# Float64 weights converted by a scaled read, a shift and an addition, and the second layer's slot stage issued straight behind the experts

## The chip, the cores and the metric

One core of a Trainium2 chip runs the whole program in one launch. The metric is device time in microseconds. The kernel before took 983.55 us as the median of 3 runs (982.73 to 985.5).

## The reference, cut to what matters

Three layers follow one another. The attention (8 batches, 8 heads, 576 tokens, 64 per head) gives x, 4608 x 512. A soft mixture of 8 experts mixes the tokens into 32 slots, runs each expert on its 4 slots, and mixes the slots back. A last layer squares its hidden values:

```
logits = x @ phi                                  # 4608 x 32
slot_input = softmax(logits, over tokens).T @ x   # 32 x 512
slot_out[e] = relu(slot_input[e] @ w1[e]) @ w2[e] # 8 experts, 512 x 1024 and 1024 x 512
y = softmax(logits, over slots) @ slot_out        # 4608 x 512
h = y @ w_in                                      # w_in 512 x 2048, float64
out = (s * relu(h)**2 + b) @ w_out                # w_out 2048 x 512, float64
```

`w_in` and `w_out` arrive in float64, so the kernel reads them as pairs of 32-bit words and makes float32 of them itself.

## The kernel before, in words

The attention runs from an order written out by hand: each step has a time `tau` in a table (`SLOT`), `at` collects the steps, and `run` issues them in the order of their times. Engines take what is issued to them in that order.

The last layer is not computed as `(c @ slot_out) @ w_in`. The kernel first forms M = slot_out @ w_in, 32 x 2048, and later h = c @ M, with c the 4608 x 32 softmax. M is called `mf` in float32, and `mst` as high and low float16 parts, with a power of two as scale. This is **M's stage** (from line 885): `slot_rows` brings the experts' sum `so` to the other axis (`sos`, `sop`, `soT`); `slots(i)` makes 256 columns of M at a time (matmul `m`, copy `part`, matmul `n` that adds four parts, copy into `mf`); then come a scale for M (`msum`), the split into `mst` (`parts`), a bound on the outputs by 16 transposes of `mf` and a maximum (`mm`, `mu`), and the scales `sk` and `bk`.

The **main loop** (from line 980) goes over 12 groups of 384 tokens and 16 slices f of 128 hidden columns: `stage_h` (matmul h, relu on ScalarE), `stage_g` (square and scale on VectorE), `stage_r` (high and low parts, ScalarE and VectorE), and `stage_o` (9 float16 matmuls of 512 columns), issued `LAG` = 4 steps behind `stage_h`. `stage_e` writes 384 rows out.

The **weights** come in 1 MB pieces, called keys: 8 of `wi` (w_in), 8 of `wo` (w_out), 16 of `w1` and 16 of `w2`. `load_w` issues a `w1` or `w2` key as two transfers of 512 KB on SyncE's queue; a load waits there until the place it goes to is free. Places: 3 (`wpost`) in the room that the attention leaves, 1 (`wright`) in the room that the routing leaves, the place of every expert key that has been used (`used`), and the places of the odd `wi` and `wo` keys once they have been converted (`split`; these loads show as `w2h`). `advance` issues a load for each place as it is named.

The **conversion** of a key is a generator: `from_f64` has three pieces, then the pieces of its `finish` list follow (one for `wi`; value, power, power2, high, low for `wo`). One call of `convert(most)` issues one piece of each conversion in flight and takes up a new one if fewer than `most` are in flight. Seven calls stand in the end of the attention's order, one behind each of the 32 expert keys, and the rest follow the experts in a loop, ahead of M's stage. The 16 keys' conversions, in order: wi0 to wi7, wo0 to wo7. The pieces are numbered below as wi2:3 for the third piece of wi2.

Of the kernel before, what the change touches and what calls it, by code (L numbers as in the profile page):

```python
# [13 lines left out]
U32 = mybir.dt.uint32  # L14
AF = mybir.ActivationFunctionType
# [25 lines left out]
def fused_kernel(  # L41
# [569 lines left out]
    def from_f64(w, pool, finish):  # L611
# [12 lines left out]
        yield  # L624
        DVE.scalar_tensor_tensor(out=f, in0=m, scalar=2.0 ** -20, in1=f, op0=ALU.mult, op1=ALU.add)
        yield
        DVE.scalar_tensor_tensor(out=e, in0=h32, scalar=-0x80000000, in1=e, op0=ALU.bitwise_and, op1=ALU.bitwise_or)
        yield
        for fn in finish:
            fn(f, e.bitcast(F32))  # L630
            yield
# [30 lines left out]
    P["cv"] = later(ph2, "cv", 2)  # L662
    wpost = places(ph2, "wpost", NPOST, reuse_waits="tile")
    ready, todo, active = set(), [], []
# [36 lines left out]
    def split_wo(i):  # L701
# [3 lines left out]
        def value(u, s):  # L705
            DVE.tensor_tensor(out=u, in0=u, in1=s, op=ALU.mult)

        def power(u, s):
            for h in range(2):
                ACT.activation(out=s[:, 512 * h:512 * h + 512], in_=u[:, 512 * h:512 * h + 512], func=AF.Abs, bias=eps,  # L710
                               accum_out=wsum[:, 2 * i + h:2 * i + h + 1])

        def power2(u, s):

            DVE.tensor_scalar(out=wpow[:, 2 * i:2 * i + 2].bitcast(I32), in0=wsum[:, 2 * i:2 * i + 2].bitcast(I32),
                              scalar1=0x7F800000, scalar2=0x7F800000, op0=ALU.bitwise_and, op1=ALU.bitwise_xor)
            ACT.mul(wpow[:, 2 * i:2 * i + 2], wpow[:, 2 * i:2 * i + 2], 2.0 ** 13)

# [9 lines left out]
        def low(u, s):  # L728
# [5 lines left out]
            if i % 2:  # L734
                empty.append(split(home["wo", i], i))
                advance()

        return from_f64(wt["wo", i], P["cv"], [value, power, power2, high, low])

    def conv_in(i):  # L740
# [3 lines left out]
        def finish(u, s):  # L744
            DVE.tensor_tensor(out=to, in0=u, in1=s, op=ALU.mult)
            have.add(i)
            if i % 2:
                empty.append(split(home["wi", i], i))
                advance()

        return from_f64(wt["wi", i], P["cv"], [finish])
# [30 lines left out]
    CMOST = 2  # L782
# [4 lines left out]
    for t in (O["rp"] - 0.01, O["rp"] - 0.005, O["tl"] + 0.1, O["re"] + 0.3, O["re"] + 0.35, O["rx"] + 0.2, O["rx"] + 0.3):  # L787
        at(z + t, 7, convert, 1)
# [12 lines left out]
    with tc.manual_schedule():  # L801
# [63 lines left out]
        while todo or active:  # L865
            convert(CMOST)
# [18 lines left out]
    with tc.manual_schedule():  # L885

        pm = ph3.enter_context(tc.tile_pool(name="pm", bufs=3, space=PSUM, reuse_waits="tile"))
        mdone = set()
        soT = e1.tile([128, 4, 32], F32, name="soT")

        def slot_rows():
# [6 lines left out]
            DVE.tensor_copy(soT, sop[:, 0:128].rearrange("p (c n) -> p c n", c=4))  # L898

        def slots(i):  # L900
# [8 lines left out]
            (DVE.tensor_copy if i % 2 else ACT.copy)(part, ps)  # L909
# [8 lines left out]
        msum = e1.tile([128, 12], F32, name="msum")  # L918
        sb_abs = e1.tile([128, 2], F32, name="sb_abs")
        ACT.activation(out=sb_abs[:, 0:1], in_=s_sb, func=AF.Abs)  # L920
        ACT.activation(out=sb_abs[:, 1:2], in_=b_sb, func=AF.Abs)
        slot_rows()
        ctrans(0, pm, "n")
        gens = [slots(i) for i in range(8)]
        for i in range(10):
            if i < 8:
                next(gens[i])
            if i >= 2:
                next(gens[i - 2], None)

        DVE.tensor_reduce(out=msum[:, 8:9], in_=msum[:, 0:8], axis=AX, op=ALU.add)
        gp = pm.tile([128, 512], F32, tag="n", name="n")
        PE.matmul(gp[:, 0:128], msum[:, 8:9].to_broadcast([128, 128]), idF, start=True, stop=True)
        DVE.tensor_reduce(out=msum[:, 9:10], in_=gp[:, 0:128], axis=AX, op=ALU.max)
        for n, x in ((10, 0x7F800000), (11, 0)):
            DVE.tensor_scalar(out=msum[:, n:n + 1].bitcast(I32), in0=msum[:, 9:10].bitcast(I32), scalar1=0x7F800000, scalar2=x,
                              op0=ALU.bitwise_and, op1=ALU.bitwise_xor)
        ACT.mul(msum[:, 10:11], msum[:, 10:11], 2.0 ** 13)
        ACT.mul(msum[:, 11:12], msum[:, 11:12], 2.0 ** -28)

        def parts(x0, x1):
            ACT.activation(out=mst[:, x0:x1], in_=mf[:, x0:x1], func=AF.Copy, scale=msum[:, 10:11])
            DVE.scalar_tensor_tensor(out=mst[64:128, x0:x1], in0=mf[64:128, x0:x1], scalar=msum[64:128, 10:11],
                                     in1=mst[64:128, x0:x1], op0=ALU.mult, op1=ALU.subtract)
            mdone.update(range(x0 // 256, x1 // 256))

        parts(0, 512)


        mt = pm.tile([128, 512], F32, tag="m", name="m")  # L950
        for f in range(16):
            PE.transpose(mt[:, 32 * f:32 * f + 32], mf[0:32, 128 * f:128 * f + 128], idF[0:32, 0:32])
# [128 lines left out]
```

## Time and profile before

| | |
|---|---|
| time, median of 3 | 983.55 us |
| profiled execution | 982.77 us |
| its span | 981.1 us, mean granted TensorE clock 0.973 |
| PE busy | 879.0 us (90%) |
| DVE busy | 703.6 us (72%) |
| ACT busy | 604.1 us (62%) |
| POOL busy | 286.5 us (29%) |

PE is TensorE's matmul, DVE VectorE, ACT ScalarE, POOL GpSimd, SP SyncE. All times count from the start of the span. A timeline row gives start, duration, engine, line, operation, output and inputs, shapes and count; in brackets, the idle time of the engine before it and what ended that. A windows row gives a stretch and its length, then each engine's busy time with its count of instructions, the granted PE clock (1.00 is full), the DMA engines' busy share, and GB/s. A groups row gives line, engine, operation, names, shapes and count, then busy time, the mean ns of one, and the idle time before them. Durations of neighbours overlap a little: two 1024-column VectorE instructions of 1.22 us start 1.14 us apart.

### The profile page before, as it was taken

To read this page: it belongs to the slowest core of one execution; us is meant where nothing else is said; L and a number is where in the kernel's file an instruction comes from. 1 tells how busy PE (TensorE), PEld (TensorE's weight loads), DVE (VectorE), ACT (ScalarE), POOL (GpSimd) and SP (SyncE) were. 2 spreads that over 40 slices of the span, in tenths; PEclk is the share of its full clock that TensorE was granted. 3 is DMA by queue.
4 is the path that set the end of the run, shared out by engine and by line. 5 is a ranking of instruction groups with operands and counts; after the bars stand their busy time and mean duration, and the time that the engine had idled before them with its cause. 6 is when DMAs were issued, how large, how long until landed. Compare 5 with 4: busy or idle time off the path is not lost.

```text
span 981.1 us, 20487 instructions
## 1 busy us (share of the span) xinstructions
PE 879.0 (90%) x8052; PEld 515.1 (53%) x8052; DVE 703.6 (72%) x1269; ACT 604.1 (62%) x1040; POOL 286.5 (29%) x224
## 2 busy tenths in 40 slices
PE   3899989988999988876785699999999999999998
PEld 2677767767777767761110334444444444444443
DVE  5798979888899879848889566565555565565553
ACT  2677767777677767753377655555555555565553
POOL 6576756665566646652000000000000000000000
PEclk9999999999999999987999789999999999999999
DMA  4544544444434434075995000001000100010001
GB/s 113 130 91 118 129 109 101 102 120 115 110 81 123 123 106 112 15 302 217 410 400 214 1 1 33 11 23 33 33 1 32 33 32 2 33 33 1 33 33 32
DMA packets 150927, 91.73 MB, mean 94 GB/s; under 512 B 127472, under 2 KB 127792, under 8 KB 150832
## 3 DMA queue, kind: packets, MB, share of 16 engines
q1 hardware_dynamic: 150832, 90.44, 30.7%
q8 instruction: 63, 1.03, 0.4%
q14 instruction: 32, 0.26, 0.1%
HBM read 80.81 MB, written 9.44 MB: 92 GB/s over the span
## 4 chain that ended last, share of the span: by engine, by line
PE 58%; DVE 21%; ACT 11%; DMA 4%; issue 3%; POOL 3%; SPq 0%; DVEq 0%; POOLq 0%; ACTq 0%
PE o L1015 13%; PE o L1014 13%; PE o L1016 13%; DVE vl L356 5%; PE s L378 4%; DVE mm L292 4%; ACT pc L383 4%; PE h L986 3%; ACT ph L255 3%; PE tp L268 2%; DMA w<-in_moe_w_dram 2%; PE s L303 2%; DVE me L292 2%; PE pv L416 1%; DVE kql L262 1%
## 5 line engine op out<-in xcount | busy, mean ns | idle before, releaser
L262 POOL TENSOR_TENSOR pl<-pc,ph 128x896 f16<-128x896 f32 (+1 forms) x128 | 232.4, 1817 | 150.0 <-ACT ph L255 82.6
L994 DVE SCALAR_TENSOR_TENSOR g<-r,sk 128x384 f32<-128x384 f32 x192 | 119.4, 622 | 128.2 <-ACT r L988 126.7
L988 ACT ACTIVATE r<-h,msum 128x384 f32<-128x384 f32 x192 | 111.4, 581 | 156.4 <-PE h L986 155.3
L383 ACT ACTIVATE pc<-s 128x896 f32<-128x896 f32 (+1 forms) x128 | 110.6, 864 | 75.1 <-PE s L378 48.0
L1002 DVE SCALAR_TENSOR_TENSOR rl<-g,bk,rh 128x384 f16<-128x384 f32 x192 | 117.9, 614 | 8.0 <-ACT rh L1000 6.7
L1000 ACT ACTIVATE rh<-g,bk 128x384 f16<-128x384 f32 x192 | 116.5, 607 | 2.2 <-DVE g L994 2.2
L255 ACT CAST ph<-pc 128x896 f16<-128x896 f32 (+1 forms) x128 | 113.4, 886 | 4.1
L292 DVE TENSOR_REDUCE mm<-s 128x2 f32<-128x1024 f32 (+3 forms) x128 | 101.8, 817 | 7.3 <-PE s L303 7.1
L766 POOL TENSOR_TENSOR c<-lgs,mc 128x192 f32<-128x192 f32 x6 | 3.0, 508 | 345.6 <-DVE mc L764 345.6
L416 PE MATMUL pv<-vh,ph 128*128 128x65 f16 x960 | 102.5, 196 | 1.2 <-DVE xt L432 1.0
L418 PE MATMUL pv<-vh,pl 128*128 128x65 f16 x960 | 101.0, 194 | 1.3 <-POOL pl L262 1.3
L417 PE MATMUL pv<-vl,ph 128*128 128x64 f16 x960 | 101.4, 193 | 0.0
L416 PEld LDWEIGHTS <-ph 128*128 128x128 f16 x960 | 86.6, 98 | 23.0 <-issue 6.3
L1016 PEld LDWEIGHTS <-rl 128*128 128x128 f16 x576 | 56.4, 98 | 68.7 <-DVE rl L1002 0.7
L1014 PEld LDWEIGHTS <-rh 128*128 128x128 f16 x576 | 56.5, 98 | 66.6 <-issue 0.3
L418 PEld LDWEIGHTS <-pl 128*128 128x128 f16 x960 | 88.7, 98 | 1.6 <-POOL pl L262 1.5
L417 PEld LDWEIGHTS <-ph 128*128 128x128 f16 x960 | 88.6, 99 | 0.0
L1015 PEld LDWEIGHTS <-rh 128*128 128x128 f16 x576 | 56.5, 98 | 58.3 <-issue 0.6
L262 DVE TENSOR_TENSOR kql<-tp,kq 128x512 fp32r<-128x512 f32 (+1 forms) x96 | 57.5, 599 | 29.2 <-ACT kq L284 28.2
L268 PE MATMUL tp<-idF,rqk 128*128 128x128 f32 x320 | 57.9, 298 | 22.0 <-DVE kql L262 9.6
L303 PE MATMUL s<-kq 64*128 64x64 f32 (+4 forms) x384 | 55.3, 336 | 20.6 <-DVE me L292 14.6
L378 PE MATMUL s<-kq 64*128 64x128 f32 (+3 forms) x384 | 70.4, 363 | 0.8
(236 smaller groups left out, 1967.7 us busy)
## 6 DMA issues: line engine op xcount, KB each, us to landing
w<-in_moe_w_dram SPq DMA_DIRECT2D x44, 512.0 KB
w2h<-in_moe_w_dram SPq DMA_DIRECT2D x20, 512.0 KB
rqk<-in_k_dram SPq DMA_DIRECT2D x64, 128.0 KB
rqk<-in_q_dram SPq DMA_DIRECT2D x64, 128.0 KB
rv<-in_v_dram SPq DMA_DIRECT2D x64, 128.0 KB
wi<-in_moe_w_in_dram SPq DMA_DIRECT2D x8, 1024.0 KB
wo<-in_moe_w_out_dram SPq DMA_DIRECT2D x8, 1024.0 KB
out_dram<-ob SPq DMA_DIRECT2D x32, 256.0 KB
```

The source lines that it names most:

```text
L255: ACT.copy(o, i)
L262: eng.tensor_tensor(out=o, in0=i, in1=h, op=ALU.subtract)
L292: DVE.tensor_reduce(out=o, in_=i, axis=AX, op=ALU.max)
L383: ACT.activation(out=pc[:, :, 0:w], in_=st.pop(("ps", p, c))[:, :, 0:w], func=AF.Exp, scale=scale)
L416: PE.matmul(o, a, vh[:, 2 * sl + h, 0:65], start=(c == 0 and n == 0), stop=False)
L417: PE.matmul(o[:, 0:64], a, vl[:, 2 * sl + h, :], start=False, stop=False)
L418: PE.matmul(o, l, vh[:, 2 * sl + h, 0:65], start=False, stop=(c == 3 and n == len(UNIT[c]) - 1))
L994: DVE.scalar_tensor_tensor(out=g0, in0=r, scalar=sk[:, f:f + 1], in1=r, op0=ALU.mult, op1=ALU.mult)
L1002: DVE.scalar_tensor_tensor(out=rl, in0=g0, scalar=bk[:, f:f + 1], in1=rh, op0=ALU.add, op1=ALU.subtract)
L1014: PE.matmul(o, rh[:, 128 * i:128 * i + 128], hl[f][0], start=(f == 0), stop=False)
L1015: PE.matmul(o, rh[:, 128 * i:128 * i + 128], hl[f][1], start=False, stop=False)
L1016: PE.matmul(o, rl[:, 128 * i:128 * i + 128], hl[f][0], start=False, stop=(f == 15))
```

## The change

`from_f64` reads the upper word as a float32 and multiplies it by 2^-112 on ScalarE, shifts the bits left by 3 and puts the sign back (VectorE); the lower word, scaled by 2^-52 in bfloat16 (ScalarE), is multiplied by the power of two of the value, taken from the upper 16 bits (VectorE); `value` or `finish` then adds the two. Up to three conversions are in flight instead of two, and two instead of one ahead of the experts, where six calls stand instead of seven. The place of an odd key is named free behind the second piece instead of the last. The loop that issued the rest of the conversions is gone: M's stage is issued behind the last expert key with `convert` between its pieces and behind it. In M's stage the 16 transposes stand behind each piece of `mf`; M's scale comes from the same maximum and minimum as the bound, by one pair of matmuls, and the sums of absolute values `msum` are gone; all `part` copies are ScalarE's; `mst` is split in pieces, most of them between the first steps of the main loop, whose first `stage_o` stand 2 to 4 steps behind `stage_h`.

```diff
-        m = pool.tile([128, n], I32, tag="cvm", name="cvm", bufs=1)
-        e = pool.tile([128, n], I32, tag="cve", name="cve")
-        f = pool.tile([128, n], F32, tag="cvf", name="cvf")
-        DVE.tensor_scalar(out=e, in0=h32, scalar1=1, scalar2=21, op0=ALU.logical_shift_left, op1=ALU.logical_shift_right)
-        DVE.tensor_scalar(out=m, in0=h32, scalar1=0xFFFFF, scalar2=None, op0=ALU.bitwise_and)
-
-        ACT.activation(out=f, in_=l32, func=AF.Copy, scale=2.0 ** -52, bias=1.0)
-        ACT.activation(out=e, in_=e, func=AF.Relu, bias=m896, scale=2.0 ** 23)
+        g = P["cv"].tile([128, n], I32, tag="cvg", name="cvg")
+        l = P["cv"].tile([128, n], BF16, tag="cvl", name="cvl")
+        e = P["cv"].tile([128, n], BF16, tag="cve", name="cve", bufs=1)
+        gf = g.bitcast(F32)
+        ACT.activation(out=gf, in_=h32.bitcast(F32), func=AF.Copy, scale=2.0 ** -112)
+        ACT.activation(out=l, in_=l32, func=AF.Copy, scale=2.0 ** -52)
         yield
-        DVE.scalar_tensor_tensor(out=f, in0=m, scalar=2.0 ** -20, in1=f, op0=ALU.mult, op1=ALU.add)
+        DVE.tensor_scalar(out=g, in0=g, scalar1=3, scalar2=None, op0=ALU.logical_shift_left)
+        DVE.scalar_tensor_tensor(out=g, in0=h32, scalar=-0x80000000, in1=g, op0=ALU.bitwise_and, op1=ALU.bitwise_or)
+        if key[1] % 2:
+            empty.append(split(home[key], key[1]))
+            advance()
         yield
-        DVE.scalar_tensor_tensor(out=e, in0=h32, scalar=-0x80000000, in1=e, op0=ALU.bitwise_and, op1=ALU.bitwise_or)
+
+        up = g.bitcast(I16).rearrange("p (n t) -> p n t", t=2)[:, :, 1]
+        DVE.tensor_scalar(out=e.bitcast(I16), in0=up, scalar1=-128, scalar2=None, op0=ALU.bitwise_and)
+        DVE.tensor_tensor(out=l, in0=l, in1=e, op=ALU.mult)
         yield
...
-            DVE.tensor_tensor(out=u, in0=u, in1=s, op=ALU.mult)
+            DVE.tensor_tensor(out=u, in0=u, in1=s, op=ALU.add)
...
-    CMOST = 2
+    CMOST = 3
...
-    for t in (O["rp"] - 0.01, O["rp"] - 0.005, O["tl"] + 0.1, O["re"] + 0.3, O["re"] + 0.35, O["rx"] + 0.2, O["rx"] + 0.3):
-        at(z + t, 7, convert, 1)
+    for t in (O["rp"] - 0.01, O["rp"] - 0.005, O["tl"] + 0.1, O["re"] + 0.3, O["rx"] + 0.2, O["rx"] + 0.3):
+        at(z + t, 7, convert, 2)
...
-        while todo or active:
-            convert(CMOST)
...
-            (DVE.tensor_copy if i % 2 else ACT.copy)(part, ps)
+            ACT.copy(part, ps)
...
-            ACT.activation(out=part, in_=ps, func=AF.Abs, bias=eps, accum_out=msum[:, i:i + 1])
-            (ACT.copy if i % 2 else DVE.tensor_copy)(mf[:, 256 * i:256 * (i + 1)], ps)
+            (DVE.tensor_copy if i < 7 else ACT.copy)(mf[:, 256 * i:256 * (i + 1)], ps)
+            yield
+            for f in (2 * i, 2 * i + 1):
+                PE.transpose(mt[:, 32 * f:32 * f + 32], mf[0:32, 128 * f:128 * f + 128], idF[0:32, 0:32])
...
+        for i in range(11):
+            for j in (i, i - 2, i - 3):
+                if 0 <= j < 8:
+                    next(gens[j], None)
+            if i < 10:
+                convert(CMOST)
+        while len(summed) < 8:
+            convert(CMOST)
...
+        extremes(0, 16)
...
+        for n in range(2):
+            PE.matmul(gp[:, 128 * n:128 * n + 128], top[:, n:n + 1].to_broadcast([128, 128]), idF, start=True, stop=True)
+        DVE.tensor_reduce(out=top, in_=gp[:, 0:256].rearrange("p (a n) -> p a n", a=2), axis=AX, op=ALU.max)
...
-        parts(512, 2048)
...
+        part_hi(0, 256)
...
+        part_lo(0, 256)
...
+        part_hi(256, 512)
...
+        at(0.9, part_lo, 256, 512)
+        for x in range(512, 2048, 512):
+            at(x / 128 - 2.6, part_hi, x, x + 512)
+            at(x / 128 - 1.8, part_lo, x, x + 256)
+            at(x / 128 - 0.8, part_lo, x + 256, x + 512)
+
+        for n in range(8):
+            at(n + 1.3, convert, CMOST)
...
-            at(n + LAG + .05, stage_o, g, f)
+            lag = min(LAG, 2 + n / 4) + .05
+            at(n + lag, stage_o, g, f)
```

## Rows read from the trace of the kernel before

**Rows 1.** Windows, by stage: first experts, second experts, conversions, M's stage, main loop.

```profile
454.30:488.50 34.20, 27.32 (x116) 4.19 (x108) 31.58 (x38) 12.54 (x11) 0.00 (x0) 0.96 1.00 397
492.00:531.40 39.40, 32.33 (x128) 4.60 (x128) 34.78 (x43) 29.04 (x51) 0.00 (x0) 1.00 0.96 368
531.40:543.20 11.80, 0.00 (x0) 0.00 (x0) 10.54 (x15) 9.05 (x17) 0.00 (x0) 0.68 0.00 0
543.20:567.30 24.10, 17.09 (x116) 8.92 (x117) 14.30 (x38) 15.07 (x42) 0.00 (x0) 0.71 0.00 1
567.30:980.00 412.70, 409.03 (x1949) 188.66 (x1947) 237.41 (x426) 228.03 (x425) 8.79 (x15) 1.00 0.07 24
```

**Rows 2.** Timeline of PE, last expert key to the first `stage_o`.

```profile
530.30 1.05 PE L853 MATMUL so<-w,hTz 128*32 128x512 f32 x4 [0.25 <-DMA w<-in_moe_w_dram]
...
543.80 1.92 PE L897 MATMUL m<-I,sos 128*128 128x32 f32 x8 [12.46 <-ACT sos L894]
...
549.64 0.64 PE L905 MATMUL m<-wi,soT 128*32 128x256 f32 x8
...
550.84 0.64 PE L905 MATMUL m<-wi,soT 128*32 128x256 f32 x8
...
558.16 1.18 PE L952 MATMUL m<-idF,mf 32*128 32x32 f32 x16
...
562.33 0.80 PE L965 MATMUL n<-idF,mu 128*128 128x128 f32 x2 [2.99 <-DVE mu L963]
...
567.33 0.63 PE L1014 MATMUL o<-wo_0s,rh 128*128 128x512 f16 x1
```

**Rows 3.** Groups of DVE by shape, 430:567 us; L994 from 600:970.

```profile
L706 DVE TENSOR_TENSOR cvf<-cvf,cve 128x1024 f32<-128x1024 f32 x8 | 9.8, 1225 | 0.3
...
L627 DVE SCALAR_TENSOR_TENSOR cve<-wo,cve 128x1024 int32<-128x1024 int32 x8 | 9.7, 1218 | 0.0
...
L619 DVE TENSOR_SCALAR cve<-wo 128x1024 int32<-128x1024 int32 x8 | 5.5, 686 | 0.0
...
L730 DVE SCALAR_TENSOR_TENSOR wo_4s<-cvf,wpow,wo_4s 128x512 f16<-128x512 f32 x4 | 2.8, 743 | 0.0
...
L994 DVE SCALAR_TENSOR_TENSOR g<-r,sk 128x384 f32<-128x384 f32 x173 | 107.5, 621 | 118.2 <-ACT r L988 116.9
```

**Rows 4.** Groups of ACT by shape, 488:560 us; L988 from 600:970.

```profile
L622 ACT ACTIVATE cvf<-wo 128x1024 f32<-128x1024 uint32 x8 | 9.2, 1152 | 0.0
...
L710 ACT ACTIVATE cve<-cvf,eps 128x512 f32<-128x512 f32 x16 | 11.3, 710 | 2.8 <-DVE cvf L706 2.8
...
L725 ACT ACTIVATE wo_4s<-cvf,wpow 128x512 f16<-128x512 f32 x4 | 2.7, 714 | 0.1
...
L988 ACT ACTIVATE r<-h,msum 128x384 f32<-128x384 f32 x173 | 100.5, 581 | 142.0 <-PE h L986 140.8
```

**Rows 5.** Timeline of DVE ahead of the experts.

```profile
442.08 0.32 DVE L509 COPY d<-s 128x160 f32<-128x160 f32 x1
...
445.19 0.75 DVE L520 SCALAR_TENSOR_TENSOR acc<-acc,f,s 128x512 f32<-128x512 f32 x1 [0.41 <-PE s L518]
...
450.82 0.35 DVE L771 TENSOR_REDUCE sc<-c 128x6 f32<-128x192 f32 x1 [2.59 <-ACT c L768]
...
451.72 0.28 DVE L808 COPY slotT<-stp 128x128 f32<-128x128 f32 x1
```

**Rows 6.** Timeline of ACT in the same stretch.

```profile
441.50 0.23 ACT L542 ACTIVATE W<-W 128x32 f32<-128x32 f32 x1 [0.58 <-DVE W L541]
```

**Rows 7.** Timeline of POOL in the same stretch.

```profile
446.90 3.02 POOL L795 MEMSET hTz<- 128x2304 f32 x1 [15.27 <-DVE ssum L527]
```

**Rows 8.** Windows of the core, the 4 us after slotT.

```profile
452.00:456.00 4.00, 3.95 (x20) 0.99 (x24) 4.00 (x5) 0.89 (x2) 1.28 (x2) 0.50 0.23 84
```

**Rows 9.** Timeline of DVE in M's stage, two reductions.

```profile
560.55 0.69 DVE L958 TENSOR_REDUCE mmax<-m 128x16 f32<-128x512 f32 x1
...
563.16 0.29 DVE L966 TENSOR_REDUCE mu<-n 128x1 f32<-128x128 f32 x1 [0.89 <-PE n L965]
```

More of the change, by code (lines that the diff above doesn't have):

```diff
@@ L661, in fused_kernel @@
     e2 = later(ctx, "e2", 2)
-    P["cv"] = later(ph2, "cv", 2)
+    P["cv"] = later(ctx, "cv", 3)
     wpost = places(ph2, "wpost", NPOST, reuse_waits="tile")
-    ready, todo, active = set(), [], []
+    ready, summed, todo, active = set(), set(), [], []
     toload = list(wseq[NPRE:])
@@ L733, in low @@
             ready.update((2 * i, 2 * i + 1))
[L734 to L738, printed above, removed]
+        return from_f64(("wo", i), [value, power, power2, high, low])
     def conv_in(i):
@@ L744, in finish @@
         def finish(u, s):
-            DVE.tensor_tensor(out=to, in0=u, in1=s, op=ALU.mult)
+            DVE.tensor_tensor(out=to, in0=u, in1=s, op=ALU.add)
             have.add(i)
[L747 to L751, printed above, removed]
+        return from_f64(("wi", i), [finish])
     def convert(most):
@@ L897, in slot_rows @@
                 PE.matmul(sop[:, 32 * c:32 * c + 32], sos[:, 128 * c:128 * c + 128], I4, start=True, stop=True)
-            DVE.tensor_copy(soT, sop[:, 0:128].rearrange("p (c n) -> p c n", c=4))
+            ACT.copy(soT, sop[:, 0:128].rearrange("p (c n) -> p c n", c=4))
         def slots(i):
@@ L917, in fused_kernel, with small @@
         mf = mstp.tile([128, 2048], F32, name="mf")
-        msum = e1.tile([128, 12], F32, name="msum")
         sb_abs = e1.tile([128, 2], F32, name="sb_abs")
-        ACT.activation(out=sb_abs[:, 0:1], in_=s_sb, func=AF.Abs)
-        ACT.activation(out=sb_abs[:, 1:2], in_=b_sb, func=AF.Abs)
+        def small(name, n=16):
+            return e1.tile([128, n], F32, name=name)
+        mm, mn, bound, gpow, sk, bk, rs_ = (small(n) for n in ("mmax", "mmin", "bound", "gpow", "sk", "bk", "rscale"))
@@ L922, in fused_kernel @@
+        top, power, inv, fm, fo = (small(n, 2) for n in ("top", "power", "inv", "fm", "fo"))
         slot_rows()
         ctrans(0, pm, "n")
-        gens = [slots(i) for i in range(8)]
[L925 to L952, printed above, removed]
-        def small(name, n=16):
-            return e1.tile([128, n], F32, name=name)
-        mm, bound, gpow, sk, bk, rs_, mu = (small(n) for n in ("mmax", "bound", "gpow", "sk", "bk", "rscale", "mu"))
-        DVE.tensor_reduce(out=mm, in_=mt.rearrange("p (f n) -> p f n", n=32), axis=AX, op=ALU.max)
+        mt = pmt.tile([128, 512], F32, name="mt")
@@ new lines, in extremes @@
+        def extremes(f0, f1):
+            x = mt[:, 32 * f0:32 * f1].rearrange("p (f n) -> p f n", n=32)
+            DVE.tensor_reduce(out=mm[:, f0:f1], in_=x, axis=AX, op=ALU.max)
+            DVE.tensor_reduce(out=mn[:, f0:f1], in_=x, axis=AX, op=ALU.min)
+        gens = [slots(i) for i in range(8)]
+        for i in range(11):
[4 more added lines that the diff above has]
+                convert(CMOST)
@@ new lines, in fused_kernel @@
+        while len(summed) < 8:
+            convert(CMOST)
+        for n, c in enumerate((s_sb, b_sb)):
+            DVE.tensor_scalar(out=sb_abs[:, n:n + 1].bitcast(I32), in0=c.bitcast(I32), scalar1=0x7FFFFFFF, scalar2=None,
+                              op0=ALU.bitwise_and)
+        DVE.tensor_scalar(out=gpow.bitcast(I32), in0=wsum.bitcast(I32), scalar1=0x7F800000, scalar2=None, op0=ALU.bitwise_and)
+        extremes(0, 16)
+        DVE.scalar_tensor_tensor(out=mn, in0=mn, scalar=-1.0, in1=mm, op0=ALU.mult, op1=ALU.max)
@@ new lines, in fused_kernel, with part_hi, part_lo @@
+        DVE.tensor_scalar(out=fm, in0=inv, scalar1=2.0 ** 13, scalar2=None, op0=ALU.mult)
+        def part_hi(x0, x1):
+            ACT.activation(out=mst[:, x0:x1], in_=mf[:, x0:x1], func=AF.Copy, scale=fm[:, 0:1])
+        def part_lo(x0, x1):
+            DVE.scalar_tensor_tensor(out=mst[64:128, x0:x1], in0=mf[64:128, x0:x1], scalar=fm[64:128, 0:1],
+                                     in1=mst[64:128, x0:x1], op0=ALU.mult, op1=ALU.subtract)
+            mdone.update(range(x0 // 128, x1 // 128))
@@ L975, in fused_kernel @@
-        DVE.tensor_scalar(out=mu[:, 3:4], in0=mu[:, 3:4], scalar1=2.0 ** -28, scalar2=None, op0=ALU.mult)
-        parts(512, 2048)
+        part_hi(256, 512)
     ph3.close()
@@ L987, in stage_h @@
             r = e3.tile([128, 384], F32, tag="r", name="r")
-            ACT.activation(out=r, in_=hps, func=AF.Relu, scale=msum[:, 11:12])
+            ACT.activation(out=r, in_=hps, func=AF.Relu, scale=fo[:, 0:1])
             rr_[g, f] = r
```

34 lines of the change are left out of this document (18 added, 16 removed).

## The prediction, made before the changed kernel ran

> **What bounds the kernel now.** I read the windows by stage first. In the main loop PE is busy 409.03 of 412.70 us at clock 1.00 while DVE and ACT have over 170 us each to spare [rows 1]; its length is fixed by its matmuls, and the change leaves those as they are. So what counts is when its first `stage_o` starts: 567.33 [rows 2]. Ahead of it lie two stretches in which PE is not the limit. Both expert halves run with the DMA engines at 0.96 to 1.00 of their time and 368 to 397 GB/s: the 32 MB of expert weights set the pace. Then PE stands still for the whole of 531.4 to 543.2, DVE busy 10.54 of 11.80, with no transfer at all; then M's stage, 24.1 us with PE busy 17.09 at a mean clock of 0.71 [rows 1]. The PE timeline says what it waited for: the last expert key ends at 531.35, and the next matmul comes at 543.80, after 12.46 us of waiting for ACT's `sos` [rows 2]. `sos` needs only `so`, which is complete at 531.35; it stands in ACT's queue behind the rest of the conversions. That wait is what the change is aimed at.
>
> **The conversions.** Per `wi` key VectorE has two one-source instructions and three two-source ones. A two-source pass over 1024 columns is 1.22 us (L706, L627), a one-source pass 0.69 (L619) [rows 3]; less the 0.08 by which neighbours overlap, 1.14 and 0.60, so 3 x 1.14 + 2 x 0.60 = 4.62 us. After: the shift 0.60, the sign 1.14, the mask on 16-bit words, the product in bfloat16, the sum 1.14. Neither the mask nor the product has a row. I bound the mask by 0.3 (half of L619, were half the bytes half the time) and 1.14, and the product by 0.66 (L730, a two-source pass over half the columns [rows 3]) and 1.14. I take 0.60 and 1.14, the rows with the same count of columns and of sources. The pair is then 1.74 (0.96 to 2.28) and the key 4.62 again: by these rows the new arithmetic saves VectorE nothing. ACT has two passes per key as before, 1.15 each [rows 4]; I take 0 for the bfloat16 output, between 0.4 gained (L710, half the columns) and nothing.
>
> No row here has both inputs in 16 bits. The Trainium skill (VectorE: DVE Perf Modes, "The perf-mode tier table") puts `tensor_tensor` on bfloat16 in SBUF at twice the float32 rate; by that the product would be 0.60 by estimate, and the time below would be 1.1 us less. The same page ("What auto-detection actually checks") gives the 16-bit packing only to steps of 1, so the mask, which reads every other word, gains nothing by its width.
>
> **What is in flight when the experts end.** Counting the calls of `convert`: before, the call behind the 32nd key issues wo2:7 and wo3:4, and wo4 to wo7 follow the experts. After, with three in flight, it issues wo6:4 and wo7:3. What is left for M's stage is wo6's and wo7's power, power2, high and low and wo7's value; all eight later calls in the loop issue nothing. Whether the engines keep up: VectorE work from the start of the experts to those pieces is six `wi` keys (27.7), six `wo` keys at 4.62 + 1.41 for low (L730 twice, overlapped) + 0.17 for power2 (37.2), wo6 4.62, wo7 3.48, some 1.0 of small things, together 74.0. One thing gets later: `hs`, between the two halves, stands in ACT's queue behind abs of wo1, which needs 27.7 + 2 x 4.62 + 1.74 of that VectorE work, so it comes at about 497, where the first half's keys are in by 458.5 + 11 x 2.64 = 487.6 (next part); before, the second half had begun by 492.0 [rows 1]. This delays PE by 5 to 7 us, not the transfers, which have free places past that point. PE's four matmuls on 512 KB take 1.05 [rows 2] against 1.32 of transfer at 397 GB/s, so over the 32 halves left it can make up 8.6. I cost it at nothing; if the places ran out, it would be up to 7.
>
> **The start of the experts.** Two conversions ahead of the experts cost something. wi1's two ACT passes (2.1) now stand between the routing's ACT work and the exponential W. ACT was idle 0.58 before W at 441.50 [rows 6], so it was free at 440.92; W starts 440.92 + 2.1 = 443.0, 1.5 late, and d, behind W on VectorE, too. d ends at 443.9 instead of 442.4 [rows 5]. Then VectorE does wi0:3 and wi1:2, 1.74 + 1.74, until 447.4, and acc comes there: 2.2 later than 445.19. POOL's clearing of hTz, which waits for the sums behind acc and lasts 3.02 [rows 7], ends at 452.1. VectorE meanwhile has wi0:4, wi1:3 and wi1:4 (4.0) from 449.0 to 453.0; then come the maximum, POOL's subtraction and ACT's exponential (1.2 in sum), so sc starts at 454.2 instead of 450.82. slotT ends 1.18 after sc's start in both: 455.4 instead of 452.0. **3.4 us late.**
>
> Against that, wi1's place is named free two pieces earlier, ahead of `wright`, and its load of one key needs only wi1:2, done at 447.4. So five keys instead of four can land before the experts start (two at 1.05 MB / 397 GB/s = 2.64 us each, 447.4 to 452.7). The load stream can only go on once the first key is used. Before, 84 GB/s in 452 to 456 [rows 8] is 0.34 MB, 0.85 us at full rate, so it resumed at 455.15, 3.1 behind slotT. After it resumes 3.4 later with 2.64 less to load. **The last expert key ends at 531.35 + 3.4 - 2.64 = 532.1.** VectorE, started at 455.4, has its 74.0 done at 529.4: hidden with 2.7 to spare. If it waits on ACT 0.7 per `wo` key, it is 3 late; wo6's abs on ACT, behind the first `part`, is needed only then, so nothing is lost.
>
> **M's stage.** `sos` 0.7 (as L710), `sop` 1.92 at half clock and so about 0.96 at full (PE comes straight from the experts at 1.00 [rows 1]), soT 0.4: first `m` at E + 2.05, with E = 532.1. `m` to `m` with an `n` between is 1.20 (549.64 to 550.84), 16 transposes 1.18 [rows 2]. PE alone would end at E + 2.05 + 9.6 + 1.2 = E + 12.8. But ACT has all the `part` copies (0.37 each), with four abs (0.71) and four high (0.71 [rows 4]) between the first four of them, some reads of sums too: part 4 comes at E + 10.2. Behind it are four `n`, one `m` and the transposes; the two pairs of low on VectorE (1.41 each) stand ahead of the copies that transposes wait for, another 0.8. I get the last transpose at **E + 15.2 = 547.3**.
>
> From there: two reductions of 0.69 instead of one, then small instructions of 0.2. Before, 560.55 to 562.33 (one reduction, five small), 0.83 to 563.16, and on [rows 9, 2]. After: 1.4 + 6 x 0.2 = 2.6 to the matmuls, 0.9, a reduction of twice the columns 0.4, three small ones 0.6, `part_hi` 0.45, `part_lo` 0.48 (a quarter of a 1024-column pass and its fixed part), h 0.5, r 0.58 and g 0.62 [rows 4, 3], and 1.2 of the second r, a `part_hi` and rh on ACT: 8.4. First `stage_o` at **555.7**, 11.6 earlier. Two h (0.17 each) then follow inside the loop that stood ahead of it before: 11.3. Later pieces of `mst` are 3 us of VectorE and 2 us of ACT over 14 steps, with over 0.9 us of slack per step [rows 1]: nothing.
>
> The sum is 982.77 - 11.3 = **971.5** on the profiled execution's time, 0.8 below the median of the runs shown; a measurement here tells about 0.3% (3 us) from no change.
>
> **Rivals.** *Conversions reach into M's stage* (0.17): with the mask and product at 1.14 each, slotT is 1.1 later and VectorE 14 x 0.54 = 7.6 more, so with the 2.7 spare gone and 3 of waits about 8 late at E; abs on ACT then holds part 1 some 5 us. 971.5 + 1.1 + 5 = 977.6. For it: VectorE was 88 to 92% busy in the experts already [rows 1]. Against: both prices at their upper ends.
>
> *The experts start no later* (0.13): if ACT's passes or VectorE's pieces find gaps I have not seen, and the key gained counts in full, 971.5 - 3.4 = 968.1; a cheaper mask and product go the same way (1.8). For it: VectorE idles 2.59 ahead of sc [rows 5]. Against: engines keep their order.
>
> *M's stage isn't freed* (0.05): VectorE's 78 us in all plus 5.6 of waits end at 540.5, and if M's pieces only come then, M without conversions takes 13.0, the rest 8.4: 561.9, so 977.4.
>
> *Slower* (0.03): VectorE's new pair at 3.3 us. It works 14 keys on it ahead of the experts' end, 22 us more, so `m`'s second piece waits till 555, and o starts at about 576: 992. It decides from about 2.7 us for the pair, above the bound of 2.28.
>
> **Chances.** The forecast with 968.5 to 974.5 has 0.60, and 0.02 is left for within 0.3%. The range 966 to 978 takes in the first three rivals. Faster 0.95, same 0.02, slower 0.03.
>
> **What would show it.** PE's wait for `sos` gone: matmul L897's successor within 2 us of the last expert key, at a clock of 1.00. slotT at 455, the last key at 532, the last transpose 15 us behind it, first `stage_o` at 556; the loop's length as before. The mask at 0.69 and the product at 1.22 or 0.69. Wrong would be: idle PE behind the experts, a product over 1.3, or a stall in the loop's first steps.

## The result and the profile after

The changed kernel takes **974.59 us** (median of 4 runs, 973.07 to 975.57) against 984.52 for the kernel before on the same chip, a ratio of 0.9899 (0.988 to 0.9917): faster by 9.9 us. The forecast was 971.5, 966 to 978. The profiled execution is the longest of the four, 975.57, where that of the kernel before was the shortest of its own; its span is 973.9 against 981.1: 7.2 less.

Busy times and the granted clock, from the page of the kernel after:

```profile
span 973.9 us, 20478 instructions
PE 874.5 (90%) x8052; PEld 515.9 (53%) x8052; DVE 700.2 (72%) x1275; ACT 599.0 (62%) x1025; POOL 285.3 (29%) x224
PEclk9799999999999999996979899999999999999999
```

No engine has noticeably less to do (PE 4.5 us less, DVE 3.4, ACT 5.1). What changed is how the work stands. The PE timeline of the kernel after, from the last expert key to the main loop (rows as in [rows 2]):

```profile
532.20 1.05 PE L859 MATMUL so<-w2h,hTz 128*32 128x512 f32 x4 [0.22 <-DMA w2h<-in_moe_w_dram]
533.94 1.08 PE L902 MATMUL m<-I,sos 128*128 128x32 f32 x8 [0.69 <-ACT sos L899]
...
541.70 0.70 PE L917 MATMUL n<-part,J 128*128 128x256 f32 x2 [0.84 <-ACT part L914]
...
549.47 0.31 PE L921 MATMUL mt<-idF,mf 32*128 32x32 f32 x2 [0.23 <-ACT mf L918]
551.57 1.62 PE L966 MATMUL n<-idF,top 128*128 128x128 f32 x4 [1.80 <-DVE top L959]
555.38 0.82 PE L999 MATMUL h<-ct,mst 128*128 128x384 f16 x2 [2.19 <-DVE mst L978]
...
558.14 0.63 PE L1027 MATMUL o<-wo_0s,rh 128*128 128x512 f16 x1
```

The 12.46 us of idle PE behind the last key [rows 2] are 0.69 now. From the last key's end (533.25) to the end of the last transpose (549.78) it is 16.5, from there to the first `stage_o` 8.4. That `stage_o` stands 9.2 earlier than before; the loop behind it is 2.0 longer (415.8 to the end of the span, 413.8 before), which leaves the 7.2.

Windows show where those 2.0 come from (columns as in [rows 1]: PE, PEld, DVE, ACT, POOL, clock, DMA share, GB/s). First those of the kernel after:

```profile
548.00:552.00 4.00, 1.98 (x11) 1.32 (x10) 2.68 (x11) 0.37 (x1) 0.00 (x0) 0.78 0.00 0
552.00:556.00 4.00, 1.78 (x6) 0.70 (x5) 2.47 (x12) 0.98 (x3) 0.00 (x0) 0.50 0.00 0
556.00:560.00 4.00, 2.33 (x7) 0.75 (x7) 3.28 (x7) 3.17 (x6) 0.00 (x0) 0.50 0.00 0
560.00:564.00 4.00, 4.00 (x12) 1.41 (x11) 1.86 (x5) 1.08 (x2) 0.00 (x0) 0.51 0.00 0
564.00:568.00 4.00, 4.00 (x21) 1.87 (x20) 1.52 (x3) 1.52 (x3) 0.00 (x0) 1.00 0.00 0
```

And one of the kernel before, whose `stage_o` starts at 567.33:

```profile
568.00:572.00 4.00, 4.00 (x16) 1.64 (x16) 3.90 (x9) 3.49 (x7) 0.00 (x0) 0.79 0.00 0
```

In the kernel after PE is busy for 1.98, 1.78 and 2.33 of 4 us; the clock falls to its lower level (0.50, 1.2 GHz) and stays there through the first 5.8 us of `stage_o`: 12 matmuls in 560 to 564, 21 in 564 to 568. In the kernel before it stays there for the first 2.4 us. Whether that belongs to the change is a question for e8.

The groups of the conversion's instructions in the kernel after (those of before are [rows 3]):

```profile
L636 DVE TENSOR_SCALAR cve<-cvg 128x1024 int16<-128x1024 int16 x16 | 12.0, 749 | 0.2
L637 DVE TENSOR_TENSOR cvl<-cvl,cve 128x1024 bf16<-128x1024 bf16 x16 | 11.1, 692 | 1.4
L629 DVE SCALAR_TENSOR_TENSOR cvg<-wo,cvg 128x1024 int32<-128x1024 int32 x8 | 9.8, 1225 | 0.3
L716 DVE TENSOR_TENSOR cvg<-cvg,cvl 128x1024 f32<-128x1024 f32 x8 | 9.8, 1221 | 0.0
```

The product takes 0.69, not the 1.22 of the other two-source passes. The attention ahead drifts by up to 5.4 us between the profiled executions, so the experiments count from a common event, the start of the routing's last maximum. It is this row in the kernel before:

```profile
439.26 0.28 DVE L292 TENSOR_REDUCE mt<-s 32x1 f32<-32x128 f32 x1 [1.17 <-PE s L482]
```

and the first row here, from the timeline of DVE and POOL in the kernel after:

```profile
440.46 0.28 DVE L293 TENSOR_REDUCE mt<-s 32x1 f32<-32x128 f32 x1 [1.17 <-PE s L483]
444.64 0.31 DVE L510 COPY d<-s 128x160 f32<-128x160 f32 x1
448.33 0.75 DVE L521 SCALAR_TENSOR_TENSOR acc<-acc,f,s 128x512 f32<-128x512 f32 x1 [0.20 <-PE s L519]
450.96 1.65 DVE L636 TENSOR_SCALAR cve<-cvg 128x1024 int16<-128x1024 int16 x1
456.02 0.35 DVE L777 TENSOR_REDUCE sc<-c 128x6 f32<-128x192 f32 x1 [1.17 <-ACT c L774]
456.92 0.28 DVE L814 COPY slotT<-stp 128x128 f32<-128x128 f32 x1
...
450.04 2.02 POOL L801 MEMSET hTz<- 128x2304 f32 x1 [17.22 <-DVE ssum L528]
```

So `slotT` starts at +16.46 (456.92 less 440.46), where before has 451.72 [rows 5], +12.46: 4.0 late.

### The profile page after: what moved, and what is told of

Read it like the earlier page. It is cut to its first block, busy times and chain, and to the rows that moved or that the text cites. A ratio compares the mean times of both kernels' runs of the same rounds, so it can differ in the third digit from the quotient of the medians.

```text
span 973.9 us, 20478 instructions
## 1 busy us (share of the span) xinstructions
PE 874.5 (90%) x8052; PEld 515.9 (53%) x8052; DVE 700.2 (72%) x1275; ACT 599.0 (62%) x1025; POOL 285.3 (29%) x224
## 2 busy tenths in 40 slices
DMA packets 150927, 91.73 MB, mean 94 GB/s; under 512 B 127472, under 2 KB 127792, under 8 KB 150832
## 4 chain that ended last, share of the span: by engine, by line
PE 52%; DVE 17%; ACT 7%; issue 2%; POOL 1%; DVEq 0%; POOLq 0%; ACTq 0%
PE o L1029 13%; PE o L1027 13%; PE o L1028 13%; PE h L999 3%; DVE vl L357 3%; PE s L379 2%; ACT pc L384 2%; DVE mm L293 2%; DVE cvg L629 2%; ACT ph L256 2%; PE tp L269 1%; DVE cve L636 1%; DVE wi L754 1%; DVE cvg L628 1%; PE pv L417 1%
## 5 line engine op out<-in xcount | busy, mean ns | idle before, releaser
L1001 ACT ACTIVATE r<-h,fo 128x384 f32<-128x384 f32 x192 | 111.1, 579 | 156.8 <-PE h L999 155.6
L379 PE MATMUL s<-mr,neg 64*128 64x128 f32 (+3 forms) x384 | 67.3, 319 | 6.8 <-DMA mr<-mT 6.5
```

The costliest lines, as they stand in the source:

```text
L379: PE.matmul(ps[:, h, o:o + c1 - c0], a[r], b[r], start=(n == 0), stop=(n == 3))
```

## The experiments

All are timed against the kernel before on the same chip (e1 to e4 on one chip, e5 to e8 on a second, e9 to e12 on a third). The five columns of places are from one profiled execution each, in us behind the maximum named above. The first `stage_o` is the first PE row whose output is `o` and whose input is `rh`; in before and e1 the 16 transposes are one row, in e4 and e6 the last two pairs are, elsewhere the last pair stands.

| kernel | slotT starts | last key ends | sos starts | last transposes start | first stage_o | median | ratio to before |
|---|---|---|---|---|---|---|---|
| before | +12.46 | +92.09 | +103.93 | +118.90 | +128.07 | 984.52 | 1 |
| after | +16.46 | +92.79 | +92.84 | +109.01 | +117.68 | 974.59 | 0.9899 (0.988 to 0.9917) |
| e1 | +12.95 | +92.89 | +103.93 | +119.41 | +128.59 | 986.13 | 1.0018 (1.0008 to 1.0028) |
| e2 | +16.49 | +92.77 | +103.20 | +119.14 | +127.82 | 984.40 | 1.0000 (0.9987 to 1.0012) |
| e3 | +15.15 | +91.78 | +91.83 | +112.16 | +134.09 | 992.71 | 1.0087 (1.0073 to 1.0101) |
| e4 | +15.10 | +91.73 | +91.84 | +112.14 | +121.46 | 976.52 | 0.9922 (0.9901 to 0.9944) |
| e5 | +15.21 | +92.18 | +98.24 | +114.86 | +123.53 | 979.07 | 0.9942 (0.9928 to 0.9955) |
| e6 | +12.80 | +91.64 | +91.68 | +111.24 | +120.57 | 973.71 | 0.9885 (0.9866 to 0.9904) |
| e7 | +16.40 | +92.49 | +92.55 | +109.08 | +117.28 | 973.28 | 0.9871 (0.9853 to 0.9888) |
| e8 | +16.64 | +92.85 | +92.90 | +109.20 | +117.87 | 972.74 | 0.9878 (0.9861 to 0.9896) |
| e9 | +16.81 | +93.03 | +98.80 | +115.33 | +123.99 | 980.55 | 0.9958 (0.9946 to 0.9970) |
| e10 | +9.89 | +86.65 | +88.10 | +105.30 | +113.50 | 970.23 | 0.9867 (0.9850 to 0.9884) |
| e11 | +16.46 | +92.91 | +92.96 | +109.00 | +117.68 | 974.73 | 0.9907 (0.9885 to 0.9929) |
| e12 | +13.03 | +92.62 | +92.67 | +108.99 | +117.19 | 972.87 | 0.9880 (0.9865 to 0.9894) |

The theory was that the gain is the order alone: `sos` no longer queues behind conversions. The rival was that cheaper conversions pay.

**e1, the new arithmetic alone**, in the kernel before.

```
-        DVE.tensor_scalar(out=e, in0=h32, scalar1=1, scalar2=21, ...)
-        DVE.tensor_scalar(out=m, in0=h32, scalar1=0xFFFFF, ...)
...
+        ACT.activation(out=gf, in_=h32.bitcast(F32), func=AF.Copy, scale=2.0 ** -112)
+        ACT.activation(out=l, in_=l32, func=AF.Copy, scale=2.0 ** -52)
...
+        DVE.tensor_tensor(out=l, in0=l, in1=e, op=ALU.mult)
```

> Before, with the new arithmetic alone (two in flight, rest of the conversions ahead of M's stage, old M's stage). Theory 'order' (the gain is that M's stage no longer waits for conversions): VectorE's key gets 0.53 us cheaper (product 0.69 instead of a 1.22 pass), on the 8 wo keys behind the stop at hs that is some 4 us, first stage_o near 563, time near 980. Rival 'arithmetic' (the cheaper passes are the gain): the whole change's 10 us, 974.6.

1.0018: nothing is gained. The first theory had expected 980 and missed too: the 4 us that it saw in the cheaper keys are not there. ACT's timeline in e1, from one pair of `wo` keys to the next:

```profile
494.14 1.20 ACT L620 ACTIVATE cvg<-wo 128x1024 f32<-128x1024 f32 x1
...
500.15 0.72 ACT L711 ACTIVATE cvl<-cvg,eps 128x512 bf16<-128x512 f32 x1 [1.65 <-DVE cvg L707]
...
504.73 0.72 ACT L711 ACTIVATE cvl<-cvg,eps 128x512 bf16<-128x512 f32 x1 [1.06 <-DVE cvg L707]
...
508.10 1.14 ACT L620 ACTIVATE cvg<-wo 128x1024 f32<-128x1024 f32 x1
```

A pair takes 13.96 us (508.10 less 494.14); in before it is 13.84. Per pair VectorE is busy for 12.54 of 13.83 us in before and for 11.45 of 13.93 in e1 (the mean of two pairs); ACT waits for VectorE's `cvg` for 1.65 and 1.06 in the rows above, and for 0.82 in before. Two engines that hand a key to and fro wait for one another, and the half microsecond saved per key on VectorE turns up as such waits.

**e2, the order undone**: the change with all conversions issued ahead of M's stage again.

```
+        while todo or active:
+            convert(CMOST)
```

> The changed kernel with the rest of the conversions issued ahead of M's stage again. Order: the two unfinished wo keys take VectorE from 530.0 to about 542, sos comes then, M's last transpose 14 us behind it at 556, first stage_o 8.4 later at 564 instead of 558: 980 to 981. Arithmetic: within 2 us of the changed kernel, 975 to 976.

The whole gain is gone (1.0000; the theory had expected 980 to 981, with a shorter M's stage). PE's row at that place in e2:

```profile
547.74 1.92 PE L904 MATMUL m<-I,sos 128*128 128x32 f32 x8 [11.05 <-ACT sos L901]
```

PE is idle for 11.05 us, much as before (12.46), and `sos` comes at +103.20. From `sos` to the first `stage_o` it is 24.6, against 24.1 before and 24.8 after: M's stage in its new form is no shorter. All of the gain, 10.4 by the table, is that it starts 11.1 earlier, less these 0.7.

**e3, the old arithmetic in the changed order.** Three of the old conversions do not fit in the room there is, so two are in flight.

```
-    P["cv"] = later(ctx, "cv", 3)
+    P["cv"] = later(ctx, "cv", 2)
-    CMOST = 3
+    CMOST = 2
```

with the old lines of `from_f64` and of `finish` put back.

> The changed kernel's order and M's stage with the old arithmetic; the old tiles have room for two in flight only, so wo4 to wo7 are issued inside M's stage and behind it. Order: M's columns are made straight behind the experts, but the bound needs the sums of wo7, so the conversions' end near 541 to 545 sets it: first stage_o 553 to 557, time 972 to 977, most of the gain kept. Arithmetic: the gain is gone, 982 to 985.

It is slower, 1.0087, which no theory had (972 to 977 was expected). `sos` comes right behind the last key, but PE stops later, in front of the main loop (PE timeline, e3):

```profile
552.84 0.41 PE L918 MATMUL mt<-idF,mf 32*128 32x32 f32 x2 [0.60 <-ACT mf L915]
566.97 1.63 PE L963 MATMUL n<-idF,top 128*128 128x128 f32 x4 [13.71 <-DVE top L956]
```

With two in flight the calls behind the 32 keys get only to wo2:8 and wo3:7. wo4 to wo7 are then issued inside M's stage, and its small VectorE instructions queue behind them: the old stop, moved from `sos` to `top`, is 13.71 us. This run alters the passes and the number in flight at once; e5 and e9 take them apart.

**e5 and e9, two in flight with enough calls**, the old arithmetic (e5) and the new (e9), otherwise the change:

```
+            if kind == "w2" and i >= 2:
+                convert(CMOST)
```

> The changed kernel's order and M's stage with the old arithmetic, two in flight, and two calls of convert behind each of the last 14 w2 keys, so that the call behind the last key issues wo6:4 and wo7:3 as in the changed kernel. Theory 'place in the queues' (what pays is that M's stage stands ahead of only two unfinished conversions; the passes' price does not, since a wo key took 6.9 us in all three orders so far): 973 to 977, all of the gain. Rival 'price' (the new arithmetic, or the third in flight, is needed for the gain): VectorE 0.53 us per key later, 7 us late at the experts' end: 979 to 984.

> As the run with the old arithmetic and two calls behind each of the last 14 w2 keys, two in flight, but with the new arithmetic. That one took 979.07. Theory 'third in flight' (with two in flight a pair of wo keys takes 13.9 us whatever the passes cost, and VectorE stands still while ACT waits at hs; only a third one in flight fills that): sos still 6 us behind the last key, 978 to 980. Rival 'price' (the cheaper product makes up the lag): 973 to 976.

0.9942 and 0.9958: the price of the passes makes no difference that could be measured here either. Both gain about half, where e5's theory had expected all of it (973 to 977) and its rival, that the price or the third in flight is needed, 979 to 984; e9 decides between the two. `sos` is 6 us behind the last key, as this row of e9 shows for PE:

```profile
538.68 1.92 PE L904 MATMUL m<-I,sos 128*128 128x32 f32 x8 [6.41 <-ACT sos L901]
```

So the third in flight is worth the other half. Why is not fully shown. At `hs`, between the halves, VectorE stands still for 5.96 us in e9 (7.08 in e1), because both conversions wait for ACT, which waits for the experts; in the kernel after the longest wait there is 3.52. But in e5 it is 3.59, and e5 is as late as e9. A pair of `wo` keys takes 14.94 us in e5 and 14.76 in e9, a microsecond more than in before.

By the tile shapes two old conversions take 20 KB per partition, as do three new ones; three old ones would take 28. So the new arithmetic's use seems to lie in its smaller buffers, which leave room for the third; three old ones in flight were not run.

**e4, the early calls moved**, so that none stands between the routing's end and `slotT`:

```
-    for t in (O["rp"] - 0.01, O["rp"] - 0.005, O["tl"] + 0.1, O["re"] + 0.3, O["rx"] + 0.2, O["rx"] + 0.3):
-        at(z + t, 7, convert, 2)
+    for t in (O["rp"] - 0.01, O["rp"] - 0.007, O["rp"] - 0.005, O["re"] + 0.3, O["rx"] + 0.6, O["rx"] + 0.7):
+        at(z + t, 7 if t < O["rx"] else 21, convert, 2)
```

> The changed kernel with the six early calls moved: the third up to before route_p, where ACT idles 6 us, and the last two behind the first step of the softmax. My reading (the start of the experts is late by two conversions' work: W behind two ACT passes, the maximum behind VectorE's pieces): slotT 3 us earlier, the load stream and the last expert key 3 us earlier, time near 971.7. Rival (the load stream resumes for another reason, or E is set by something else): 974.6, no change.

0.9922 (976.52), no better than the change, where 971.7 was expected. `slotT` is only 1.36 earlier, and M's stage is stretched. PE's timeline in e4 shows both:

```profile
454.74 1.92 PE L813 MATMUL stp<-W,acc 128*128 128x32 f32 x8 [8.04 <-DVE lgs L533]
...
542.11 1.22 PE L917 MATMUL n<-part,J 128*128 128x256 f32 x2 [0.84 <-ACT part L914]
...
543.61 1.08 PE L910 MATMUL m<-wi,soT 128*32 128x256 f32 x8
```

`stp` waits for the copy of the last routing's scores (`lgs`), which VectorE takes late. And `n` takes 1.22 where after has 0.70: in this execution the clock fell inside M's stage, which the kernel after went through at 1.00.

**e6, one conversion ahead of the experts** instead of two:

```
-    for t in (O["rp"] - 0.01, O["rp"] - 0.005, O["tl"] + 0.1, O["re"] + 0.3, O["rx"] + 0.2, O["rx"] + 0.3):
-        at(z + t, 7, convert, 2)
+    for t in (O["rp"] - 0.01, O["rp"] - 0.005, O["tl"] + 0.1, O["re"] + 0.3, O["re"] + 0.35, O["rx"] + 0.2, O["rx"] + 0.3):
+        at(z + t, 7, convert, 1)
```

> The changed kernel with one conversion in flight ahead of the experts, seven calls as before. My reading of the start: slotT 3.4 to 4 us earlier behind the routing, but wi1's place comes late for a key ahead of the experts, 2.6 back: the experts' end 1 us earlier, the conversions one piece behind; 973.5 to 975. Rival (the second conversion ahead of the experts costs or gives more than that): beyond 972 to 977.

0.9885, the same as the change within the intervals. `slotT` is 3.66 earlier, the last key 1.15. From the last key's end to the end of the last transposes it is 4.0 longer (20.6 against 16.5), at this clock in e6:

```profile
536.00:540.00 4.00, 2.44 (x18) 1.27 (x22) 2.50 (x6) 2.89 (x10) 0.00 (x0) 0.81 0.00 0
540.00:544.00 4.00, 4.00 (x22) 1.51 (x17) 3.17 (x6) 3.08 (x8) 0.00 (x0) 0.50 0.00 0
```

Two causes were possible, the clock itself or the piece that one conversion fewer ahead leaves over for M's stage; e12 tells them apart.

**e7, PE kept busy**: the change with 38 more matmuls that nothing reads, at four places where PE waits between `sos` and the loop.

```
+            for k, j in enumerate((i, i - 2, i - 3)):
+                if i in (3, 4) and k:
+                    spin(dm, 3)
...
+        spin(dm, 8)
...
+        spin(dm, 10)
...
+        at(1.2, spin, ps_o.tile([128, 512], F32, tag="o0", name="o0"), 8)
```

> The changed kernel with 38 added matmuls on PE that nothing reads (128x512 f16: 12 between the pieces of M's stage, 8 ahead of the bound's matmuls, 10 behind them, 8 behind the second h). Theory: the first 5.6 us of stage_o ran at a granted clock of 0.5, because PE had been mostly idle from 549.8 to 558.1; kept busy it stays at 1.00, which gives 2.8 there, 0.8 at the bound's matmuls and 0.4 at h: 970.5 to 971. Rival: the added matmuls only delay those behind them, 975 to 976.

Two of the windows of e7:

```profile
552.00:556.00 4.00, 3.63 (x18) 1.69 (x18) 2.66 (x13) 1.24 (x3) 0.00 (x0) 1.00 0.00 0
...
560.00:564.00 4.00, 4.00 (x20) 1.85 (x19) 2.61 (x6) 2.17 (x4) 0.00 (x0) 1.00 0.01 4
```

The clock is 1.00 from the last key into the loop, 20 matmuls stand in 560 to 564 instead of 12, and the span behind the first `stage_o` is 413.3 instead of 415.8 (971.2 less 557.88). These 2.5 us are between two executions. In the medians the gain is not shown: 973.28 lies between what theory (970.5 to 971) and rival (975 to 976) expected, the ratio, 0.9871, overlaps with that of the change by a little, and e8, without the added matmuls, took 972.74 on the same chip.

**e8, places named free behind the last piece again**:

```
-        if key[1] % 2:
-            empty.append(split(home[key], key[1]))
-            advance()
...
+            if fn is finish[-1] and key[1] % 2:
+                empty.append(split(home[key], key[1]))
+                advance()
```

> The changed kernel, with the places of odd keys named free behind the last piece of their conversion, as before. My reading: one key fewer lands ahead of the experts (2.6 us), later ones come in time: experts' end 2.6 us later, 977. Rival (the early place does nothing): 974.6.

0.9878, and the last key ends at +92.85 as after (+92.79): the earlier naming does nothing here, since with two conversions ahead the last piece of wi1 too is issued before the experts.

e8 shows something else as well. From the last transposes to the first `stage_o` (556.53) its PE does what it does in the kernel after, in the same 8.67 us. Its windows:

```profile
552.00:556.00 4.00, 0.82 (x2) 0.13 (x2) 2.77 (x12) 2.60 (x6) 0.00 (x0) 0.50 0.00 0
556.00:560.00 4.00, 3.74 (x12) 1.39 (x13) 3.38 (x7) 1.56 (x3) 0.00 (x0) 0.63 0.00 0
560.00:564.00 4.00, 4.00 (x21) 1.86 (x19) 2.29 (x4) 2.17 (x4) 0.00 (x0) 1.00 0.00 0
```

The clock is at 0.50 for 2.4 us of `stage_o`, as in before, and not for 5.8; the span behind the first `stage_o` is 414.1. In the 8 us ahead of `stage_o` PE is busy for 2.68 in before, after and e8 alike, so a lack of work there does not explain the 5.8. The span behind the first `stage_o` in the other runs without added matmuls: 414.1 in e2 and e9, 414.3 to 414.5 in e3, e5 and e6, 415.6 in e4, 415.7 in e11, and 415.0 in e1, which has M's stage of the kernel before and the clock at 0.50 for 5.1 us. It differs from one execution to the next.

**e11 and e12**: the change once more, and e6 and e7 together (both edits as above).

> The changed kernel itself, to stand beside the others on the same chip: 973 to 976 by either theory.

> The changed kernel with the 38 added matmuls and one conversion in flight ahead of the experts. Its run without the matmuls fell to a clock of 0.5 inside M's stage in the profile (19.6 us from the last key to the last transpose). If the clock was the cause: M's stage at 16 to 17 us again, and with the experts' end 1 us earlier 970 to 972. If it was the missing piece of conversion: M's stage stays near 19, 973 to 975.

e11 repeats the change (0.9907; every step of the table within 0.12). e12 has `slotT` as early as e6 and its clock held; from the last key's end to the end of the transposes it is back to 16.7 us. So the clock had stretched it in e6, not the piece left over. Its median, 972.87, lies between the two expectations; the trace decides, not the time.

**e10, the best version**: e7 with e4's calls, and the last routing's copy of the scores ahead of `stp`.

```
-        at(z + O["rn"], 9, route_n, b)
+        at(z + (O["rx"] + 0.01 if b == NB - 1 else O["rn"]), 9, route_n, b)
```

> The changed kernel with the 38 added matmuls, the early calls moved as in the run that moved them, and the routing's last copy (lgs), for which stp waited there, issued right behind acc. Clock at 1.00 into the loop gives 2.5 (as measured in the traces before), slotT at 13 us instead of 16.5 behind the routing's last maximum gives up to 3: 968.5 to 971. If the start of the experts doesn't set their end: 971.5 to 973, as the run with added matmuls alone.

970.23 us, a ratio of 0.9867, against 974.73 for the change on the same chip (e11): faster than both kernels. The timelines of DVE and PE in e10:

```profile
445.87 0.31 DVE L533 COPY lgs<-s 128x160 f32<-128x160 f32 x1
...
448.57 0.27 DVE L814 COPY slotT<-stp 128x128 f32<-128x128 f32 x1
...
446.23 1.92 PE L813 MATMUL stp<-W,acc 128*128 128x32 f32 x8 [2.50 <-DVE lgs L533]
...
524.28 1.05 PE L859 MATMUL so<-w2h,hTz 128*32 128x512 f32 x4 [0.19 <-DMA w2h<-in_moe_w_dram]
```

With `lgs` copied early `slotT` starts at +9.89, 6.6 ahead of the change, and here, with two conversions still ahead, the last key follows by nearly as much, 6.1. At the first `stage_o` 4.2 of these are left: `sos` stands behind conversions once more, 1.45 behind the last key, and the clock is at 0.50 for 3.4 us of M's stage.

## Why the prediction was right, and where its sizes were off

**The aim.** The wait for `sos` went, and e2 shows that without this nothing is gained. The chain named in the prediction (`sos` behind conversions in ACT's queue) is right. The rivals "the experts start no later" and "M's stage isn't freed" did not come: `slotT` is 4.0 late, `sos` 0.05 behind the last key.

**The conversions.** "The new arithmetic saves VectorE nothing" came out right in the time, by another way. The mask takes 0.69 in 15 of 16 cases, as taken (the group's mean, 749 ns, holds one of 1.65); the product is 0.69, where the row of the two-source float32 pass gave 1.22. The Trainium skill (VectorE: DVE Perf Modes, "The perf-mode tier table") had the bfloat16 product at twice the float32 rate, and this trace agrees (0.692 against 1.221). A key is therefore 0.5 cheaper than the 4.62 of the sum, and e1, and e5 beside e9, show that this is worth nothing: a `wo` key takes 6.9 us with the old passes (13.84 for two in before), with the new (13.96 in e1) and with three in flight, where ACT's rows in the kernel after are 20.8 apart for three:

```profile
508.04 1.17 ACT L625 ACTIVATE cvg<-wo 128x1024 f32<-128x1024 f32 x1
...
528.85 1.13 ACT L625 ACTIVATE cvg<-wo 128x1024 f32<-128x1024 f32 x1
```

**What is in flight.** The count of calls was right, and e3 beside e5 shows that it decides: fewer pieces issued ahead, and the change is slower than before by the mechanism of the "slower" rival, small instructions of M queued behind conversions. The prediction saw that only as a matter of prices. VectorE was to be done at 529.4; it was not: by DVE's timeline in the kernel after, wo6 only began at

```profile
530.01 0.69 DVE L628 TENSOR_SCALAR cvg<-cvg 128x1024 int32<-128x1024 int32 x1 [0.23 <-ACT cvg L625]
```

since summing VectorE's work left out the waits on ACT beyond the 0.7 per key that were allowed. From `slotT` to the product of wo7 (456.92 to 537.88) VectorE is busy for 70.0 of 81.0 us, where the sum had 74.0 of work and at most 5.6 of waits. So "conversions reach into M's stage" came in part, by the waits and not by the prices that the rival named.

**`hs`** was put at 497, 5 to 7 late and free of cost. It came at 499.42; the wait is this one among those of the kernel after (total, count, longest):

```profile
PE htp L848 <- ACT hs L845: 8.4, 1, 8.4
```

The last key is where the transfers put it all the same: right.

**The start of the experts.** 3.4 late was predicted for `slotT`, 4.0 measured; POOL's clearing of `hTz` can account for the 0.6, since it stretched a mask from 0.69 to 1.65 (below). The last key was predicted 0.75 late (3.4 less a key's 2.64) and is 0.70 late, which is luck in part: both terms came out some 0.6 larger. The reason given for the second term is wrong: by e8 it is not the early naming of wi1's place that lets one more key land, but that all of wi1 is converted ahead of the experts. Its size is borne out only roughly: with one conversion ahead `slotT` is 3.4 to 3.7 earlier than after, and the last key only 0.2 (e12) and 1.15 (e6).

**M's stage.** From the last key to the last transpose 15.2 was predicted and 16.5 measured. PE's waits there are for copies that stand behind conversions in the queues of ACT and VectorE (0.84 for `part` in the rows above); no run shows that these are the whole 1.3. The 8.4 from there to `stage_o` were measured as 8.4.

**The main loop.** "The loop's length as before", but for two h, did not hold in the profile: it is 2.0 longer. The clock was at half for the first 2.4 us of `stage_o` before and for 5.8 after; half of the difference is 1.7, and the two `h` that moved into the loop are 0.34. Only the two `h` can be put down to the change: in e8, e2 and e9 the loop is 0.3 longer than before, as was forecast, and e1, with the old order, is 1.3 longer at half the clock for 5.1 us. The prediction worked out the 8.4 of small instructions and did not ask at which clock the loop behind them starts; the runs show that this differs between executions, by up to 1.7 us, and why stays open.

**The sum.** The first `stage_o` was to come 11.6 earlier; it comes 10.4 earlier behind the common event (1.3 of M's stage), and 9.2 on the span's own scale, since the attention of this execution is 1.2 later. The medians differ by 9.9; the forecast had 12 against the median of 983.55 that it knew. The measured 974.59 is inside the range, but 0.1 above the band of 968.5 to 974.5 to which 0.60 was given.

## What to carry to other kernels

In an engine's queue, count what is issued ahead of the one instruction that everybody waits for: the order, with enough work in flight, was worth 10 us here, cheaper instructions beside it nothing, as two engines that pass work to and fro only wait longer for each other. What a cheaper form frees in memory may matter more than the time it saves. And a short serial stretch can have a second price, the clock behind it: look at the granted clock of the stretch that follows. Matmuls that nothing reads held it here and shortened the loop by 0.8 to 2.5 us from trace to trace, too little to show in the medians. Before you put such a difference down to a change, look for it in a second execution.

## What the hardware showed that was not expected

- **VectorE and POOL exclude each other in some instructions.** The mask beside POOL's clearing of `hTz` took 1.65 us and ended 0.55 behind it (452.61 and 452.06 in the rows above); in e4 it took 1.39 and ended 0.54 behind the clearing, in e10 1.16 and 0.55. In the kernel before it was the other way about: one-source passes of VectorE ran until 447.96, and the clearing, begun at 446.90, took 3.02 [rows 7] instead of 2.02, so it ended 1.96 behind them. A two-source pass beside the clearing (449.40 in e5) kept its 1.20. The Trainium skill (SBUF — State Buffer, "SBUF: two separate sides") has a port pair that the two engines lock for a whole instruction, and these rows agree with it. The last of the one-source passes in the kernel before:

```profile
447.29 0.67 DVE L620 TENSOR_SCALAR cvm<-wi 128x1024 int32<-128x1024 int32 x1
```

- **The clock differs between executions at the same place.** In e4 PE was busy 2.94 of the 4 us from 536 and the clock fell in the next 4; the kernel after was busy 2.79 in the same 4 and kept 1.00 until 548. At the start of the loop the same work ahead of it left 2.4 us at half clock in e8 and 5.8 in the kernel after. The spread of the runs fits: e4 lies between 973.8 and 980.4, with mean clocks from 0.973 to 0.960. What decides it is left open.
